# Recurrent attention and squared-ReLU FFN: stated issue order, two first solves stated side by side, inverses stored from GpSimd's queue

## The chip, the cores and the metric

The kernel runs on one core of a Trainium2 chip. The metric is the device time of one execution in microseconds (us), as a median of several runs. Every run has a state, fast or slow; verdicts here use fast runs alone. Each chip job ran the kernel before on the same chip beside the kernels under test, and its median lay between 1529.9 and 1535.5 us in all of them, so times of different jobs can be set side by side to about 0.3%.

## The reference

Attention of 4 sequences, 8 heads, 768 steps and head size 40, with a state that decays and is corrected at every step, and then an FFN over all 3072 tokens:

```python
# r, k, v, w, a, b: (4, 8, 768, 40) float32
for t in range(S):
    y[:, :, t] = einsum('bhd,bhde->bhe', rt, state)
    Sa = einsum('bhde,bhe->bhd', state, at)
    state = state * wt[:, :, None, :] - einsum('bhd,bhe->bhde', Sa, bt)
    state = state + einsum('bhd,bhe->bhde', vt, kt)
# tokens x: (3072, 320); moe_w_in: (320, 2048), moe_w_out: (2048, 320), float64
h = np.maximum(x @ w_in, 0.0)
return h * h @ w_out
```

The kernel cuts time into 6 rounds of 128 steps; a round has 4 chunks, one per sequence, 24 in all. A chunk has an early part (decays, and the matrix N of how steps correct each other), a remaining part (the products that don't need the state), and a chain (the state's part, which needs an inverse T built from N). The inverses of a round are found together in one "solve", a loop of 63 steps on 128 lanes. The FFN is woven into the chunks. The weights come as float64 and are unpacked to float32 on VectorE in 24 pieces of w_in and 16 of w_out.

## The kernel before

The solve takes an engine as argument: round 0's runs on VectorE, all others on GpSimd. Its loads and the store of the inverse are issued from SyncE, like nearly all transfers; the raw weights are fetched from ScalarE's queue.

```python
def solve(c, eng):
    ns = new("half_n", [128, HC, HC], 1)            # one buffer
    ts = new("half_t", [128, HC // 2, HC], 1)
    # ... clear ts, set its diagonal
    for par in range(2):
        for bb in range(B):
            for half in range(2):                    # 16 loads
                nc.sync.dma_start(out=ns[at:at + H], in_=kept_n[c * B + bb][rows, :, rows]...)
    yield
    for s in range(HC - 1):                          # 63 steps, two operations each
        eng.tensor_tensor(p_, ns[:, s, s + 1:]..., ts[:, :n, s:s + 1]..., Alu.mult)
        eng.tensor_tensor(ts[:, :n, s + 1:], ts[:, :n, s + 1:], p_, Alu.subtract)
        yield
    for par in range(2):
        nc.sync.dma_start(out=dst, in_=ts[par * 64:(par + 1) * 64])   # kept_t[c]
    yield
```

```python
# chain(i, g), first lines, when there is a state already
nc.vector.tensor_tensor(f_[:, :, 0], ended[bb], g["ends"][:, 0], Alu.mult)
nc.vector.tensor_copy(f_[:, :, 1], f_[:, :, 0])
nc.vector.tensor_tensor(f_, f_, same, Alu.mult)
nc.vector.tensor_tensor(st[:, :, :, :D], st[:, :, :, :D], f_..., Alu.mult)   # scale the state
for q in range(NP):
    nc.tensor.transpose(p_[...], st[:, q]..., ident)
```

```python
# the main loop
for i in range(len(order)):
    parts = [(chain(i, ready.pop(i)), 10)]
    # ... load(i + 1), rest(i + 1), the early part of chunk i + 8, weights, FFN steps
    weave(*parts)
    if bb == B - 1 and c + 2 < NCH:
        run(solve(c + 2, nc.gpsimd))
```

The order in which this is written isn't the order of issue: a scheduler moves instructions on each engine. So the weights, stated in the loop, are unpacked from 21 us on, before chunk 0.

## Time and profile before

| | before |
|---|---|
| median of 3 runs | 1534.52 us (1530.77 to 1537.87) |
| profiled span, granted clock | 1532.3 us, 0.786 |
| TensorE (PE) busy | 1062.4 us, 69% |
| VectorE (DVE) busy | 598.7 us, 39% |
| GpSimd (POOL) busy | 566.7 us, 37% |
| share of the chain that ended last | GpSimd 36%, TensorE 32% |

No engine is full. A busy share is a mean over stages with different limits.

### The profile page before, as it was taken

To read this page: it belongs to the slowest core of one execution; us is meant where nothing else is said; L and a number is where in the kernel's file an instruction comes from. 1 tells how busy PE (TensorE), PEld (TensorE's weight loads), DVE (VectorE), ACT (ScalarE), POOL (GpSimd) and SP (SyncE) were. 2 spreads that over 40 slices of the span, in tenths; PEclk is the share of its full clock that TensorE was granted. 3 is DMA by queue.
4 is the path that set the end of the run, shared out by engine and by line. 5 is a ranking of instruction groups with operands and counts; after the bars stand their busy time and mean duration, and the time that the engine had idled before them with its cause. 6 is when DMAs were issued, how large, how long until landed. Compare 5 with 4: busy or idle time off the path is not lost.

```text
span 1532.3 us, 18790 instructions
## 1 busy us (share of the span) xinstructions
PE 1062.4 (69%) x7248; PEld 884.2 (58%) x7248; DVE 598.7 (39%) x1330; ACT 202.1 (13%) x453; POOL 566.7 (37%) x702
## 2 busy tenths in 40 slices
PE   3300025009975989649989769899399994499999
PEld 2200014008854878537878658788278784388877
DVE  5887699604623243212135321346031342022311
ACT  0000001001210211101202101112012111021211
POOL 2110000009990079920199700499500899100000
PEclk9555555556897996859967878959799887699999
DMA  9634694374606677063846185654447640422100
GB/s 172 153 69 88 100 163 89 62 58 88 111 1 125 64 133 130 0 114 64 90 85 116 25 135 61 79 112 77 84 81 61 102 77 2 79 63 50 29 11 9
DMA packets 389881, 123.01 MB, mean 80 GB/s; under 512 B 318752, under 2 KB 372896, under 8 KB 389792
## 3 DMA queue, kind: packets, MB, share of 16 engines
q1 hardware_dynamic: 384000, 111.32, 45.6%
q10 hardware_dynamic: 5792, 10.49, 3.1%
q8 instruction: 57, 0.93, 0.3%
q14 instruction: 32, 0.26, 0.1%
HBM read 79.00 MB, written 41.78 MB: 79 GB/s over the span
## 4 chain that ended last, share of the span: by engine, by line
POOL 36%; PE 32%; DMA 11%; DVE 10%; SPq 7%; issue 4%; ACTq 0%; ACT 0%; DVEq 0%; POOLq 0%
PE ps_f L77 19%; POOL half_t L270 19%; POOL half_p L268 17%; PE ps_c L77 8%; PE ps_w L77 2%; DMA raw<-in_moe_w_in_dram 2%; SPq L262 2%; DMA in_k<-in_k_dram 2%; DMA raw<-in_moe_w_out_dram 2%; DVE half_t L270 2%; DVE half_p L268 2%; PE ps_w L202 2%; SPq L274 1%; SPq L398 1%; DMA kept_down<-down 1%
## 5 line engine op out<-in xcount | busy, mean ns | idle before, releaser
L268 POOL TENSOR_TENSOR half_p<-half_n,half_t 128x462 f32<-128x462 f32 (+46 forms) x315 | 255.6, 811 | 397.3 <-DMA in_k<-in_k_dram 176.1
L270 POOL TENSOR_TENSOR half_t<-half_t,half_p 128x462 f32<-128x462 f32 (+46 forms) x315 | 281.7, 894 | 24.7
L77 PE MATMUL ps_f<-tokens,w_in 128*128 128x256 f32 x1152 | 288.3, 399 | 0.5 <-DVE hid L416 0.5
L77 PEld LDWEIGHTS ps_f<-tokens,w_in 128*128 128x128 f32 x1152 | 217.7, 197 | 34.0 <-issue 1.5
L77 PE MATMUL ps_f<-w_out,hid 128*128 128x320 f32 x768 | 220.7, 441 | 0.0
L416 DVE TENSOR_TENSOR hid<-ps_f,hid 128x256 f32<-128x256 f32 x192 | 81.2, 423 | 319.2 <-ACT hid L415 319.0
L77 PEld LDWEIGHTS ps_f<-w_out,hid 128*128 128x128 f32 x768 | 144.4, 192 | 57.4 <-issue 3.0
L202 PE MATMUL ps_w<-ident,in_k 128*128 128x128 f32 x96 | 20.1, 342 | 151.0 <-DMA in_k<-in_k_dram 150.9
L77 PE MATMUL ps_c<-xr,T 64*64 64x40 f32 x768 | 65.8, 249 | 81.4 <-DMA T<-kept_t 74.5
L415 ACT ACTIVATE hid<-ps_f 128x256 f32<-128x256 f32 x192 | 73.6, 383 | 346.5 <-PE ps_f L77 346.5
L77 PEld LDWEIGHTS ps_c<-xr,T 64*64 64x64 f32 x768 | 59.1, 159 | 96.4 <-DMA T<-kept_t 75.0
L202 PEld LDWEIGHTS ps_w<-ident,in_k 128*128 128x128 f32 x96 | 14.2, 178 | 155.0 <-DMA in_k<-in_k_dram 117.7
L202 PE MATMUL ps_w<-ident,in_w 128*128 128x128 f32 x96 | 22.2, 376 | 113.9 <-DMA in_w<-in_w_dram 109.6
L77 PE MATMUL ps_w<-aT,bT 40*128 40x128 f32 x384 | 41.1, 352 | 76.3 <-DVE aT L239 76.3
L229 DVE TENSOR_TENSOR_SCAN up<-ps_w,ones 128x64 f32<-128x64 f32 x96 | 26.2, 273 | 170.9 <-PE ps_w L202 169.3
L253 POOL MEMSET half_t<- 128x2048 f32 x5 | 9.0, 1809 | 217.2 <-DMA kept_t<-half_t 217.2
L77 PEld LDWEIGHTS ps_w<-aT,bT 40*128 40x128 f32 x384 | 33.7, 244 | 86.0 <-issue 75.8
L202 PEld LDWEIGHTS ps_w<-ident,in_w 128*128 128x128 f32 x96 | 16.4, 199 | 115.5 <-issue 111.2
L244 ACT COPY N<-ps_w 128x512 f32<-128x512 f32 x48 | 25.8, 589 | 351.0 <-PE ps_w L77 284.0
L376 DVE TENSOR_TENSOR state<-ps_c,state 128x320 f32<-128x320 f32 x20 | 9.8, 491 | 126.2 <-PE ps_c L77 126.2
L218 DVE TENSOR_TENSOR RV<-ps_w,upper 128x512 f32<-128x512 f32 x48 | 30.9, 683 | 64.1 <-PE ps_w L77 64.1
L77 PEld LDWEIGHTS ps_c<-in_v,A 128*128 128x128 f32 x384 | 52.6, 215 | 2.4 <-ACT kvT L297 1.0
(182 smaller groups left out, 1475.2 us busy)
## 6 DMA issues: line engine op xcount, KB each, us to landing
kept_n<-N SPq DMA_DIRECT2D x48, 256.0 KB
half_n<-kept_n SPq DMA_DIRECT2D x96, 128.0 KB
kept_down<-down SPq DMA_DIRECT2D x24, 258.0 KB
kept_up<-up SPq DMA_DIRECT2D x24, 258.0 KB
kept_a<-aT SPq DMA_DIRECT2D x24, 256.0 KB
down<-kept_down SPq DMA_DIRECT2D x24, 256.0 KB
up<-kept_up SPq DMA_DIRECT2D x24, 256.0 KB
kept_t<-half_t SPq DMA_DIRECT2D x12, 512.0 KB
```

What stands on the lines that cost most here:

```text
L77: nc.tensor.matmul(o, l_, r_, start=start, stop=True, skip_group_check=True)
L202: nc.tensor.transpose(p_[:, q * 128:(q + 1) * 128], pair(x_, q), ident)
L218: nc.vector.tensor_tensor(t_, p_, over4(upper), Alu.mult)
L229: nc.vector.tensor_tensor_scan(up[:, q, MID + 1:C + 1], wT[:, q, MID:], ones, 1.0, Alu.mult, Alu.mult)
L244: nc.scalar.copy(t_, p_)
L262: nc.sync.dma_start(out=ns[at:at + H], in_=kept_n[c * B + bb][rows, :, rows].rearrange("s h t -> h s t"))
L268: eng.tensor_tensor(p_, ns[:, s, s + 1:].unsqueeze(1).to_broadcast([128, n, m_]), ts[:, :n, s:s + 1].to_broadcast([128, n, m_]), Alu.mult)
L270: eng.tensor_tensor(ts[:, :n, s + 1:], ts[:, :n, s + 1:], p_, Alu.subtract)
L274: nc.sync.dma_start(out=dst, in_=ts[par * 64:(par + 1) * 64])
L398: nc.sync.dma_start(out=t_[row:row + m_, j], in_=t_[at:at + m_, NT])
L415: nc.scalar.activation(h_, p_, Act.Relu)
L416: nc.vector.tensor_tensor(h_, p_, h_, Alu.mult)
```

## The change

The intent: every engine issues in the order in which the program states it, so that the author and not the scheduler decides what comes ahead of what; solves 0 and 1 are stated side by side (VectorE and GpSimd); the weights move from before chunk 0 into chunks 0 to 2; and the inverse is stored from GpSimd's own queue, so that SyncE doesn't wait for GpSimd. The core of the diff:

```diff
+    ctx.enter_context(tc.manual_schedule())
...
+    raws = [single(f"raw{i}", [128, WP, 2]) for i in range(2)]
+    def fetch_weights():
+        dst, srcs, cleared = pieces.pop(0)
+        raw = raws[len(pieces) % 2].bitcast(I32)[:, :dst.shape[-1]]
+        if cleared:
+            nc.gpsimd.memset(raws[len(pieces) % 2], 0.0)
         for row, m_, src in srcs:
             nc.scalar.dma_start(out=raw[row:row + m_]..., in_=src.bitcast(I32))
+        fetched.append((dst, raw))
...
-        ns = new("half_n", [128, HC, HC], 1)
+            ns = [new("half_n0", [128, Q, HC], 1), new("half_n1", [128, Q, Q], 1)]   # 32 loads, not 16
...
-        for par in range(2):
-            nc.sync.dma_start(out=dst, in_=ts[par * 64:(par + 1) * 64])
+        nc.gpsimd.dma_start(out=kept_t[c].rearrange(...), in_=flat)
...
-    weave((solve(0, nc.vector), HC + 1), (several(range(B, LEAD), prepare), 4 * B))
-    run(solve(1, nc.gpsimd))
-    run(rest(0, ready[0]))
+    # ... the 8 early parts, each a step ahead of the next
+    load(0)
+    fetch_weights()
+    first = rest(0, ready[0])
+    solving = [solve(0, nc.vector), solve(1, nc.gpsimd)]
+    for s_ in solving:
+        next(s_)                      # the loads of both
+    for _ in range(6):
+        next(first)
+    for s_ in solving:
+        run(s_)
+    run(first)
```

Smaller parts: decays are kept and loaded with their ends, T is loaded in 4 pieces, and a raw buffer is cleared only the first times a piece doesn't fill it (`cleared`).

More of the change, by code (lines that the diff above doesn't have):

```diff
@@ L137, with rounded @@
         nc.gpsimd.memset(same[e * DP:(e + 1) * DP, :, e:e + 1], 1.0)
-    middle = lambda t_: t_[:, :, MID:MID + 1]
-    ups = Ring("up", 1, [128, NP, C + 2], 1.0, middle)
-    downs = Ring("down", 1, [128, NP, C + 2], 1.0, middle)
+    whole = lambda t_: t_
+    ups = Ring("up", 2, [128, NP, C + 2], 1.0, whole)
+    downs = Ring("down", 2, [128, NP, C + 2], 1.0, whole)
     minus_x = Ring("minus_x", 2, [128, H, DP], 0.0, pads)
-    states = Ring("state", B, [128, NP, 2, DP], 0.0, lambda t_: t_)
+    states = Ring("state", B, [128, NP, 2, DP], 0.0, whole)
     w_in = single("w_in", [128, NT, DFF])
     w_out = single("w_out", [128, NF, DM])
-    def rounded(dst, srcs):
-        raw = work.tile([128, WP, 2], I32, tag="raw", name="raw")[:, :dst.shape[-1]]
-        n = 128
-        if sum(m_ for _, m_, _ in srcs) < n:
-            nc.gpsimd.memset(raw, 0)
+    WP = 320
+    WI = 256
+    raws = [single(f"raw{i}", [128, WP, 2]) for i in range(2)]
+    fetched = []
+    def fetch_weights():
+        if not pieces:
+            return
+        dst, srcs, cleared = pieces.pop(0)
+        raw = raws[len(pieces) % 2].bitcast(I32)[:, :dst.shape[-1]]
+        if cleared:
+            nc.gpsimd.memset(raws[len(pieces) % 2], 0.0)
         for row, m_, src in srcs:
             nc.scalar.dma_start(out=raw[row:row + m_].rearrange("p f e -> p (f e)"), in_=src.bitcast(I32))
+        fetched.append((dst, raw))
+    def rounded(dst, raw):
+        n = 128
         lo, hi = raw[:, :, 0].bitcast(U32), raw[:, :, 1]
@@ L172, in rounded, with weights @@
         nc.vector.tensor_tensor(dst, dst, rest, Alu.add)
-    WP = 320
-    WI = 256
-    pieces = [(w_in[:, j, f:f + WI], [(row, n, moe_w_in[o:o + n, f:f + WI]) for j_, row, o, n in places if j_ == j])
-              for f in range(0, DFF, WI) for j in range(NT)]
-    pieces += [(w_out[:, f, :], [(0, 128, moe_w_out[f * 128:(f + 1) * 128, :])]) for f in range(NF)]
-    def load_weights(n):
-        for _ in range(min(n, len(pieces))):
-            dst, srcs = pieces.pop(0)
-            if moe_w_in.dtype != FP32:
-                rounded(dst, srcs)
-                continue
-            if sum(m_ for _, m_, _ in srcs) < 128:
-                nc.gpsimd.memset(dst, 0.0)
-            for row, m_, src in srcs:
-                nc.scalar.dma_start(out=dst[row:row + m_], in_=src)
+    pieces = []
+    for j in range(NT):
+        for f in range(0, DFF, WI):
+            srcs = [(row, n, moe_w_in[o:o + n, f:f + WI]) for j_, row, o, n in places if j_ == j]
+            pieces.append((w_in[:, j, f:f + WI], srcs, f < 2 * WI and sum(n for _, n, _ in srcs) < 128))
+    pieces += [(w_out[:, f, :], [(0, 128, moe_w_out[f * 128:(f + 1) * 128, :])], False) for f in range(NF)]
+    def weights(n):
+        for _ in range(n):
+            if moe_w_in.dtype == FP32:
+                if pieces:
+                    dst, srcs, _ = pieces.pop(0)
+                    if sum(m_ for _, m_, _ in srcs) < 128:
+                        nc.gpsimd.memset(dst, 0.0)
+                    for row, m_, src in srcs:
+                        nc.scalar.dma_start(out=dst[row:row + m_], in_=src)
+            else:
+                fetch_weights()
+                if fetched:
+                    rounded(*fetched.pop(0))
+            yield
     kept_n = [dram.tile([C, H, C], FP32, tag=f"n{i}", name=f"kept_n{i}") for i in range(len(order))]
@@ L196 @@
     kept_down = [dram.tile([128, NP, C + 2], FP32, tag=f"dn{i}", name=f"kept_down{i}") for i in range(len(order))]
-    kept_t = [dram.tile([B, 2, H, HC, HC], FP32, tag=f"t{c}", name=f"kept_t{c}") for c in range(NCH)]
+    kept_t = [dram.tile([2, B, 2, H, HC // 2, HC], FP32, tag=f"t{c}", name=f"kept_t{c}") for c in range(NCH)]
     def turn(x_):
@@ L227, in early @@
         wT = turn(x_["w"])
+        yield
         for q in range(NP):
@@ L231, in early @@
         yield
+        bT_, aT_ = turn(x_["b"]), turn(x_["a"])
         nc.vector.reciprocal(down[:, :, MID + 1:C + 1], up[:, :, MID + 1:C + 1])
         nc.vector.reciprocal(up[:, :, :MID], down[:, :, :MID])
-        nc.sync.dma_start(out=kept_up[i][:, :, :C + 1], in_=up[:, :, :C + 1])
-        nc.sync.dma_start(out=kept_down[i][:, :, :C + 1], in_=down[:, :, :C + 1])
+        nc.sync.dma_start(out=kept_up[i], in_=up)
+        nc.sync.dma_start(out=kept_down[i], in_=down)
         yield
         bT, aT = turned("bT", 1), turned("aT", 1)
-        nc.vector.tensor_tensor(bT, turn(x_["b"]), down[:, :, 1:C + 1], Alu.mult)
-        nc.vector.tensor_tensor(aT, turn(x_["a"]), up[:, :, :C], Alu.mult)
+        nc.vector.tensor_tensor(bT, bT_, down[:, :, 1:C + 1], Alu.mult)
+        nc.vector.tensor_tensor(aT, aT_, up[:, :, :C], Alu.mult)
         nc.sync.dma_start(out=kept_a[i], in_=aT)
@@ L250, in solve @@
     def solve(c, eng):
-        ns = new("half_n", [128, HC, HC], 1)
-        ts = new("half_t", [128, HC // 2, HC], 1)
+        Q = HC // 2
+        if c > 0:
+            ns = [new("half_n0", [128, Q, HC], 1), new("half_n1", [128, Q, Q], 1)]
+            ts, prod = new("half_t", [128, Q, HC], 1), new("half_p", [128, 528], 1)
+        else:
+            room = w_out.rearrange("p f c -> p (f c)")
+            ns = [room[:, :Q * HC].rearrange("p (s t) -> p s t", s=Q),
+                  room[:, Q * HC:Q * HC + Q * Q].rearrange("p (s t) -> p s t", s=Q)]
+            ts = room[:, Q * HC + Q * Q:2 * Q * HC + Q * Q].rearrange("p (j t) -> p j t", j=Q)
+            prod = w_in[:, NT - 1, :528]
         eng.memset(ts, 0.0)
@@ L260, in solve @@
                 for half in range(2):
-                    rows = slice(half * HC, (half + 1) * HC)
-                    nc.sync.dma_start(out=ns[at:at + H], in_=kept_n[c * B + bb][rows, :, rows].rearrange("s h t -> h s t"))
+                    for n_, part in enumerate(ns):
+                        rows = slice(half * HC + n_ * Q, half * HC + (n_ + 1) * Q)
+                        cols = slice(rows.start, (half + 1) * HC)
+                        nc.sync.dma_start(out=part[at:at + H], in_=kept_n[c * B + bb][rows, :, cols].rearrange("s h t -> h s t"))
                     at += H
@@ L266, in solve @@
             n, m_ = s // 2 + 1, HC - 1 - s
-            p_ = new("half_p", [128, 528], 1)[:, :n * m_].rearrange("p (j t) -> p j t", j=n)
-            eng.tensor_tensor(p_, ns[:, s, s + 1:].unsqueeze(1).to_broadcast([128, n, m_]),
+            p_ = prod[:, :n * m_].rearrange("p (j t) -> p j t", j=n)
+            eng.tensor_tensor(p_, ns[s // Q][:, s % Q, s % Q + 1:].unsqueeze(1).to_broadcast([128, n, m_]),
                               ts[:, :n, s:s + 1].to_broadcast([128, n, m_]), Alu.mult)
@@ L271, in solve @@
             yield
-        for par in range(2):
-            dst = kept_t[c].rearrange("b f h (j two) t -> (b f h) two j t", two=2)[:, par]
-            nc.sync.dma_start(out=dst, in_=ts[par * 64:(par + 1) * 64])
+        nc.gpsimd.dma_start(out=kept_t[c].rearrange("two b f h j t -> (two b f h) (j t)"), in_=flat)
         yield
@@ L280, in rest @@
         x_ = loaded.pop(i)
-        up, down, aT = turned("up", 2), turned("down", 1), turned("aT_", 2)
-        ends = g["ends"] = new("ends", [128, 2, NP], 2)
-        nc.sync.dma_start(out=down, in_=kept_down[i][:, :, 1:C + 1])
+        up, down = new("up", [128, NP, C + 2], 2), new("down", [128, NP, C + 2], 1)
+        aT = turned("aT_", 2)
+        nc.sync.dma_start(out=down, in_=kept_down[i])
         nc.sync.dma_start(out=aT, in_=kept_a[i])
-        nc.sync.dma_start(out=up, in_=kept_up[i][:, :, :C])
-        with nc.allow_non_contiguous_dma(reason="two decays a head and channel"):
-            nc.sync.dma_start(out=ends[:, 0], in_=kept_down[i][:, :, 0])
-            nc.sync.dma_start(out=ends[:, 1], in_=kept_up[i][:, :, C])
+        nc.sync.dma_start(out=up, in_=kept_up[i])
+        ends = g["ends"] = new("ends", [128, NP], 3)
         g["up"], g["aT"] = up, aT
+        yield
         kT, rT = turned("kvT", 1), turned("rT", 2)
-        nc.vector.tensor_tensor(kT, turn(x_["k"]), down, Alu.mult)
+        nc.vector.tensor_tensor(kT, turn(x_["k"]), down[:, :, 1:C + 1], Alu.mult)
+        nc.vector.tensor_copy(ends, down[:, :, 0])
         yield
@@ L303, in rest @@
         for q in range(NP):
-            nc.tensor.transpose(p_[:, q * 128:(q + 1) * 128], down[:, q], ident)
+            nc.tensor.transpose(p_[:, q * 128:(q + 1) * 128], down[:, q, 1:C + 1], ident)
         inv = p_.rearrange("t (h d) -> t h d", h=H)[:, :, :D]
@@ L312, in rest @@
         g["T"], g["N"] = new("T", [128, H, HC], 2), new("N21", [HC, H, HC], 2)
+        nc.sync.dma_start(out=g["N"], in_=kept_n[i][:HC, :, HC:])
         for half in range(2):
-            nc.sync.dma_start(out=g["T"][half * HC:(half + 1) * HC], in_=kept_t[c][bb, half].rearrange("h j t -> j h t"))
-        nc.sync.dma_start(out=g["N"], in_=kept_n[i][:HC, :, HC:])
+            for par in range(2):
+                nc.sync.dma_start(out=g["T"][half * HC + par:(half + 1) * HC:2],
+                                  in_=kept_t[c][par, bb, half].rearrange("h j t -> j h t"))
         yield
@@ L328, in chain @@
             f_ = new("f", [128, NP, 2], 2)
-            nc.vector.tensor_tensor(f_[:, :, 0], ended[bb], g["ends"][:, 0], Alu.mult)
+            nc.vector.tensor_tensor(f_[:, :, 0], ended[bb], g["ends"], Alu.mult)
             nc.vector.tensor_copy(f_[:, :, 1], f_[:, :, 0])
@@ L377, in chain @@
             ended[bb] = new(f"end{bb}", [128, NP], 2)
-            nc.vector.tensor_copy(ended[bb], g["ends"][:, 1])
+            nc.vector.tensor_copy(ended[bb], g["up"][:, :, C])
             yield
@@ L394, in chain @@
         t_ = tokens[i // GB][:, :, n * C:(n + 1) * C]
-        nc.vector.tensor_tensor(t_, y_, g["up"], Alu.mult)
+        nc.vector.tensor_tensor(t_, y_, g["up"][:, :, :C], Alu.mult)
         for j, row, h, d, m_ in gaps:
@@ L405, in ffn @@
         for gi in range(len(order) // GB):
-            while gi not in gathered:
+            while gi not in gathered or len(pieces) + len(fetched) > NF:
                 yield False
@@ L418, in ffn @@
                 yield True
+            while pieces or fetched:
+                yield False
             for n in range(GB):
@@ L435 @@
     gathered = set()
-    PER_CHUNK = -(-(NF + 4 * GB) // GB)
+    STEPS = NF + 4 * GB
     def run(gen):
@@ L450, in weave @@
             run(gen)
-    def several(n, f):
-        for i in n:
-            if i < len(order):
-                yield from f(i)
     def prepare(i):
@@ L460, in prepare, with filler @@
         yield from early(i)
-    def weights(n):
-        while n:
-            load_weights(1)
-            n -= 1
+    def filler(n):
+        for _ in range(n):
+            next(second, None)
             yield
-    def filler(n):
-        while n and next(second):
-            n -= 1
-            yield
+    firsts = [prepare(i) for i in range(LEAD)]
+    for i in range(LEAD + 1):
+        if i == 0:
+            next(firsts[0]), next(firsts[0])
+            continue
+        now, then = firsts[i - 1], firsts[i] if i < LEAD else iter(())
+        next(now)
+        next(then, None)
+        next(now)
+        next(then, None)
+        run(now)
     ready = {0: {}}
-    run(several(range(B), prepare))
     load(0)
-    weave((solve(0, nc.vector), HC + 1), (several(range(B, LEAD), prepare), 4 * B))
-    run(solve(1, nc.gpsimd))
-    run(rest(0, ready[0]))
+    fetch_weights()
+    first = rest(0, ready[0])
[7 more added lines that the diff above has]
+    run(first)
     for i in range(len(order)):
@@ L484 @@
             ready[i + 1] = {}
-            parts.append((rest(i + 1, ready[i + 1]), 6))
+            parts.append((rest(i + 1, ready[i + 1]), 7))
         if i + LEAD < len(order):
-            parts.append((prepare(i + LEAD), 4))
-        if pieces:
-            parts.append((weights(20), 20))
-        parts.append((filler(PER_CHUNK), PER_CHUNK))
+            parts.append((prepare(i + LEAD), 5))
+        if pieces or fetched:
+            n = len(pieces) + len(fetched) - NF if i < GB else NF
+            n = -(-n // (GB - i)) if i < GB else n
+            parts.append((weights(n), n))
+        parts.append((filler(STEPS // GB + 1), STEPS // GB + 1))
         weave(*parts)
```

## The prediction

> **What bounds the kernel now.** I read the page first, then the chain that ended last, then tables by stretch, then the timelines of SyncE's queue, VectorE and TensorE. From the page, the chain's shares by engine:
>
> ```profile
> POOL 36%; PE 32%; DMA 11%; DVE 10%; SPq 7%; issue 4%; ACTq 0%; ACT 0%; DVEq 0%; POOLq 0%
> ```
>
> GpSimd, busy for 37% of the span, carries as much of the chain as TensorE, busy for 69%. So no engine is full: the two take turns. The table by stretch shows where (span, busy us of PE, PEld, DVE, ACT, POOL, granted clock, DMA share, GB/s):
>
> ```profile
> 76.00:197.50 121.50, 5.15 (x28) 3.96 (x28) 94.44 (x283) 1.07 (x2) 6.62 (x13) 0.50 0.49 91
> 197.50:293.50 96.00, 28.99 (x168) 25.19 (x168) 90.28 (x196) 5.98 (x11) 0.00 (x0) 0.53 0.52 99
> 293.50:344.00 50.50, 0.00 (x0) 0.00 (x0) 0.00 (x0) 0.00 (x0) 2.11 (x3) 0.50 0.76 71
> 552.00:638.00 86.00, 81.00 (x634) 69.16 (x634) 41.49 (x79) 16.64 (x37) 79.96 (x78) 0.84 0.51 97
> 638.00:672.00 34.00, 0.04 (x1) 0.00 (x0) 0.42 (x1) 0.61 (x2) 20.38 (x34) 0.54 0.28 51
> 1318.00:1484.00 166.00, 161.72 (x1204) 132.16 (x1204) 39.97 (x76) 31.44 (x72) 0.00 (x0) 0.96 0.22 46
> ```
>
> Until 294 us VectorE is the bound (early parts, weights, solve of round 0). Then all wait 50 us for the store of the inverse, the loads for the next solve, and T. From 344 us the rounds repeat (GpSimd's solves end at 461, 659, 874, 1092, 1310): period about 217 us, in which TensorE runs well, then dry. SyncE's queue says why (start, us, what):
>
> ```profile
> 603.42 0.65 SPq L314 DMA_DIRECT2D T<-kept_t  x1
> 658.65 2.71 SPq L274 DMA_DIRECT2D kept_t<-half_t  x2
> ```
>
> For 55 us the queue stands on the inverse's store, which waits for GpSimd; every later load is behind it. The loads of a solve hold the queue too, 31.22 / 14 = 2.23 us each (2.41 in the quiet stretch at 298 us):
>
> ```profile
> 500.30 31.22 SPq L262 DMA_DIRECT2D half_n<-kept_n  x14
> ```
>
> In the tail, without solves, TensorE is full at clock 1.00, and a chunk takes 35.5 us from one decay transpose to the next:
>
> ```profile
> 1383.21 0.66 PE L304 MATMUL ps_w<-ident,down 128*128 128x128 f32 x4
> 1418.66 0.65 PE L304 MATMUL ps_w<-ident,down 128*128 128x128 f32 x4
> ```
>
> **What the Trainium skill says.** SBUF — State Buffer, "Who interferes with whom": a VectorE instruction with two SBUF inputs contends with a GpSimd instruction that reads SBUF, and the loser waits the whole instruction out. The trace agrees: the same two-input operation on 8 elements, without and with a solve on GpSimd:
>
> ```profile
> 247.94 0.15 DVE L331 TENSOR_TENSOR f<-f,same 128x8 f32<-128x8 f32 x1
> 358.33 0.69 DVE L331 TENSOR_TENSOR f<-f,same 128x8 f32<-128x8 f32 x1
> ```
>
> Around 358 us such operations lose 0.41 to 0.54 us each, at 417 up to 0.85; I take 0.56. DMA: Bandwidth & Descriptors, "Why a DMA increments its semaphore by 16 and not by 1": the outermost dimension sets how many of the 16 DMA engines serve a transfer; these loads have 8 (heads). The DMA share of 0.52 to 0.8 beside them fits. The same page, "Anatomy of one DMA — SWDGE (gpsimd) path": about 2.0 us + bytes / 436e3 from GpSimd's queue; for the 1 MB inverse an estimate of 4.4 us. The trace of before has no large transfer from there. TensorE: Matmul & The Clock Gate, "What's actually happening": idle halves the clock until some microseconds of work; agrees (0.54 in the dry stretch, 1.00 in the tail).
>
> **The change part by part**, from the instruction streams of the changed kernel, built but not run.
>
> *Early parts, 8 chunks.* VectorE per chunk: 8 scans 1.5 us, 2 reciprocals 3.3, 2 products 1.3 = 6.1 (5.4 to 11.4 us of before). A chunk moves about 1.8 MB; at the 162 to 212 GB/s that before shows when its DMA is full, 8.5 to 11 us; its packets are longer now (2 KB rows for decays), so I take 8.4, DMA-bound: 8 x 8.4 + 8 = 76 us.
>
> *Loads of both solves.* Each 64x64 load is split in two, to skip a quarter of it: 64 loads, of as many rows as the 32 before. Estimate from 2.23 to 2.41 us per pair, a little off for shorter rows: 2.1 x 32 = 68 us. In SyncE's order they all stand before the first decay load of chunk 0's remaining part, and in VectorE's order that part's six products stand before the solve. So the solve can't start before 76 + 3 + 68 = 148 us plus that part's chain (5 matrix steps at the cold clock, copies, masks), 14 us: 162 us.
>
> *Solves.* On VectorE: busy 64.93 us in 126 operations, and 0.035 between two: 69 us, to 231. The "side by side" does not come about: in GpSimd's order the store of round 0's inverse, which waits for VectorE, stands before the first operation of round 1's solve. So GpSimd starts at 231, not beside it. Store (4.4 + its issue) and T loads: 9 us; chunk 0 begins at 240 us, against 344.
>
> *Weights.* They now lie in chunks 0 to 2, on VectorE, beside GpSimd's solve. A w_in piece takes 2.8 us (20.76 to 23.57), of which four operations have two SBUF inputs: 2.8 + 4 x 0.56 = 5.0. Twelve a chunk and about 13 us of VectorE's other work. Two pieces precede chunk 0's wait: to 249 us; then 10 x 5.0 + 13 = 63, to 312; chunk 1: 12 x 5.0 + 14 = 74, less 7 since the solve (117 us + about 15 for the contention) ends at 366: 379. Chunk 2: 16 w_out pieces at 3.3 = 53, + 13, + 16 x 0.42 of the FFN, + 4 for late fetches: 77, to 456. Chunk 3 is TensorE's, 38: 494. Before had ended chunk 3 near 455, so here the change is behind by some 40 us.
>
> *Rounds 1 to 5.* A chunk on TensorE: 35.5 (tail) + 2.3 for an early part (12 transposes, 16 small products) = 38 us where there is one, 35.5 where not. The store no longer holds SyncE. But in stated order the 32 loads of solve c+2 stand at each round's start, after T and before the next chunk's k: 34 us + 1 + 5 (k and decays landing), in which TensorE has some 6 us of chain and FFN work. 34 + 6 - 6 + 1 for re-warming = 35 us dry, at four starts (after chunks 3, 7, 11, 15). A round: 4 x 38 + 35 = 187 us against 217. GpSimd's loop: loads 37, solve 117 + 5, store 6, T 4 = 169 < 187: not the bound.
>
> *Sum.* 494 + 12 x 38 + 8 x 35.5 + 4 x 35 = 1374. Tail: the last two chunks' FFN, 38.4 us at full clock (96 x 0.217 + 64 x 0.274, tail of before), and 6 for latency and the output: 1418, say **1420 us**.
>
> **The rivals.** (1) *TensorE isn't dry at the round starts*, if SyncE gets ahead of it: 4 x 35 away, 1280. For it: before ran on for 40 us beyond such loads. Against: there the scheduler put FFN work in between; the stated order has matrix work of the next chunk's k first. (2) *The weights cost more*: if every two-input operation waits out a full GpSimd operation (1.1 us at mid-solve) and fetches come late behind ACT's copies, chunks 0 to 2 take 60 us more: 1480. For it: waits of 0.85 us at mid-solve. Against: the mean of all is lower. (3) *Strict order costs TensorE a wait at many steps*, which halves the clock too: 42 instead of 38 us a chunk, 1500, as good as the same. For it: the clock fell to 0.66 in parts of 570 to 600 us. Against: the tail ran a like order full. (4) *GpSimd's loop becomes the bound*, if split loads cost per load: 64 x 2.23 at start (+75), and 71 a round: period 206: together +150, slower than before. Against: a load of half the rows has half the descriptors per DMA engine.
>
> **Range and chances.** The terms that may err: weights +-35, the dry starts -60/+40, chunk length 20 x -1/+3, start +-20. They are partly independent: 1345 to 1500. Faster by over 2% means below 1504: 0.86. Within 2%: 0.10. Slower: 0.04.
>
> **What would show each step.** T of chunk 0 landing near 240 us; GpSimd's first solve operation after the store, not near 150; VectorE's two-input weight operations at about 1 us while GpSimd solves, 0.42 after; VectorE nearly full in chunks 0 to 2, TensorE not, to about 456; SyncE's queue in 32 loads of about 1.06 us at four round starts, with TensorE dry for about 35 us; rounds of 187 us; no stretch in which SyncE stands on the store. It is wrong if the rounds take 210 us or more, if TensorE's clock stays under 0.8 in them, or if the weights run past 500 us.

## The result, and the profile after

| | before | after |
|---|---|---|
| median | 1532.64 us (4 runs, 1528.92 to 1537.87) | 1606.67 us (4 runs, 1602.88 to 1609.7) |
| ratio | | 1.0479, 95% interval 1.0438 to 1.052 |
| profiled span, clock | 1532.3 us, 0.786 | 1608.0 us, 0.787 |

The kernel became slower by nearly 5%. A ratio is the mean time of one kernel's fast runs over that of the other's fast runs of the same rounds, so it isn't quite the ratio of the medians.

On the page, the chain that ended last has changed hands (shares of the span by engine):

```profile
PE 52%; issue 15%; DVE 10%; SPq 9%; POOL 8%; DMA 5%; ACT 0%; ACTq 0%; DVEq 0%; POOLq 0%
```

(SPq and ACTq are the queues from which SyncE and ScalarE issue transfers.) GpSimd fell from 36% to 8%: it no longer sets the rounds. The time was lost in other places, and three of them can be read off the trace.

**The start.** In the table by stretch (span, then busy us of PE, PEld, DVE, ACT, POOL, granted clock, DMA share, GB/s) there is a stretch in which GpSimd alone works:

```profile
240.00:312.00 72.00, 0.00 (x0) 0.00 (x0) 0.00 (x0) 0.00 (x0) 67.06 (x64) 0.50 0.00 0
```

The prediction had VectorE full of weights there and chunk 0 ending at 312 us. T had come early, and solve 1 had begun right behind the store (timelines of GpSimd and of TensorE: start, us, engine, line, operation; `w_out` here is round 0's inverse, as its solve works in the room of weights that aren't unpacked yet):

```profile
216.59 0.68 POOL L305 DMA_DIRECT2D kept_t<-w_out  x1 [204.66 <-DVE power L176]
217.35 0.29 POOL L301 TENSOR_TENSOR half_p<-half_n,half_t 128x63 f32<-128x63 f32 x1
...
224.26 1.90 PE L78 MATMUL ps_c<-xr,T 64*64 64x40 f32 x16 [76.58 <-DMA T<-kept_t]
```

The timeline of all engines at the end of that solve shows what the others were waiting for:

```profile
334.22 0.60 POOL L305 DMA_DIRECT2D kept_t<-half_t  x1 [0.31 <-POOL half_t L303]
334.81 0.65 POOL L165 MEMSET raw<- 128x640 f32 x1
335.50 2.81 ACTq L167 DMA_DIRECT2D raw<-in_moe_w_in_dram  x4
338.35 0.42 ACT L387 COPY minus_x<-ps_c 64x320 f32<-64x320 f32 x1 [190.22 <-DMA raw<-in_moe_w_in_dram]
338.82 1.92 PE L78 MATMUL ps_c<-minus_x,N 64*64 64x40 f32 x16 [111.63 <-ACT minus_x L387]
```

Read it from below. TensorE stood 112 us for a copy of ScalarE. ScalarE stood because the fetch of a weight piece is ahead of that copy in its order. The fetch stood because the second raw buffer had to be cleared first. The clearing takes 0.65 us, on GpSimd, and is stated behind the whole of solve 1; VectorE waits for the piece. The Trainium skill says of the queues in PSUM — Partial Sum Buffer, "Engine vs sequencer instructions": "ScalarE/VectorE/GpSimdE queues are strict FIFO." The trace agrees: 0.65 us of work came 117 us late, and three engines stood for it.

**The round starts.** SyncE's queue at the start of a round, and TensorE in the same stretch:

```profile
562.63 2.59 SPq L347 DMA_DIRECT2D T<-kept_t  x4
...
566.47 28.87 SPq L295 DMA_DIRECT2D half_n<-kept_n  x32
595.45 0.88 SPq L114 DMA_DIRECT2D in_k<-in_k_dram  x1
```

```profile
PE ps_w L221 <- DMA in_k<-in_k_dram: 121.3, 6, 29.4
```

The second fence is from the list of waits (us in total, times, longest). TensorE waits up to 29.4 us for the next chunk's k, because 32 loads of a later solve are ahead of it. This is as predicted.

**Every chunk's start.** TensorE's timeline at the start of a chunk inside a round, and the waits on the line that scales the state:

```profile
900.76 0.67 PE L78 MATMUL ps_f<-tokens,w_in 128*128 128x256 f32 x2 [1.87 <-DMA tokens<-tokens]
...
906.63 0.95 PE L369 MATMUL ps_c<-ident,state 128*128 128x128 f32 x4 [3.44 <-DVE state L365]
```

```profile
  PE ps_c L369: 49.7, 20
```

In stated order the scaling stands on VectorE behind products of the FFN (`hid`), which wait for TensorE, which waits for a gather of tokens. So VectorE reaches the scaling late, and TensorE stands for it once a chunk: 49.7 us in 20 times, and the granted clock falls after such a stand (here to 0.50 from 908 to 910 us, and back to 1.00 from 912).

| end of chunk (its product with the decays, us) | predicted | after |
|---|---|---|
| 0, 1, 2, 3 | 312, 379, 456, 494 | 376, 433, 505, 557 |
| length of chunks 4, 5, 6, 7 | 73, 38, 38, 38 | 71, 49, 43, 51 |
| 23, and the end | 1374, 1418 | 1562, 1608 |

A round takes 214 us (chunks 4 to 7), and the last weight piece is unpacked from 518 us on: two of the prediction's three signs of being wrong, "210 us or more" and "past 500 us".

### The profile page after: what moved, and what is told of

Same layout as the page of the kernel before. It is cut to its first block, busy times and chain, and to the rows that moved or that the text cites. A ratio compares the mean times of both kernels' runs of the same rounds, so it can differ in the third digit from the quotient of the medians.

```text
span 1608.0 us, 18792 instructions
## 1 busy us (share of the span) xinstructions
PE 1052.2 (65%) x7248; PEld 866.0 (54%) x7248; DVE 601.0 (37%) x1354; ACT 201.0 (13%) x453; POOL 562.9 (35%) x692
## 4 chain that ended last, share of the span: by engine, by line
PE 52%; issue 15%; DVE 10%; SPq 9%; POOL 8%; DMA 5%; ACT 0%; ACTq 0%; DVEq 0%; POOLq 0%
PE ps_f L78 29%; PE ps_c L78 13%; SPq L295 7%; PE ps_w L78 5%; POOL half_t L303 4%; POOL half_p L301 3%; PE ps_w L221 3%; DMA in_k<-in_k_dram 2%; SPq L431 1%; DMA raw<-in_moe_w_in_dram 1%; DMA tokens<-tokens 1%; DVE signed L180 1%; PE ps_c L369 1%; DVE power L184 1%; DMA raw<-in_moe_w_out_dram 1%
## 5 line engine op out<-in xcount | busy, mean ns | idle before, releaser
L78 PE MATMUL ps_f<-tokens,w_in 128*128 128x256 f32 x1152 | 326.1, 431 | 46.0 <-DMA tokens<-tokens 25.6
L78 PEld LDWEIGHTS ps_f<-tokens,w_in 128*128 128x128 f32 x1152 | 234.4, 215 | 90.9 <-DVE hid L449 22.1
L78 PE MATMUL ps_c<-minus_x,N 64*64 64x40 f32 x384 | 29.3, 237 | 111.7 <-ACT minus_x L387 111.6
L321 DVE TENSOR_TENSOR kvT<-ps_w,down 128x512 f32<-128x512 f32 x24 | 16.6, 691 | 221.0 <-DMA down<-kept_down 142.6
L78 PEld LDWEIGHTS ps_c<-minus_x,N 64*64 64x64 f32 x384 | 26.4, 145 | 121.5 <-ACT minus_x L387 112.5
L176 DVE TENSOR_SCALAR power<-raw 128x256 int32<-128x256 int32 (+1 forms) x40 | 11.8, 296 | 130.1 <-DMA raw<-in_moe_w_in_dram 127.1
L78 PE MATMUL ps_c<-in_v,A 128*128 128x40 f32 x384 | 59.0, 324 | 0.0
L237 DVE TENSOR_TENSOR A<-ps_w,upper 128x512 f32<-128x512 f32 x48 | 30.9, 685 | 72.2 <-PE ps_w L78 72.2
L78 PE MATMUL ps_w<-rT,kvT 40*128 40x128 f32 x384 | 33.5, 310 | 32.4 <-DVE RX L237 31.6
L369 PE MATMUL ps_c<-ident,state 128*128 128x128 f32 x80 | 17.9, 364 | 49.7 <-DVE state L365 49.7
```

The lines of the kernel that those rows point to most:

```text
L78: nc.tensor.matmul(o, l_, r_, start=start, stop=True, skip_group_check=True)
L237: nc.vector.tensor_tensor(t_, p_, over4(upper), Alu.mult)
L321: nc.vector.tensor_tensor(kT, turn(x_["k"]), down[:, :, 1:C + 1], Alu.mult)
L369: nc.tensor.transpose(p_[:, q * 128:(q + 1) * 128], st[:, q].rearrange("p e d -> p (e d)"), ident)
```

## The experiments

Twelve kernels ran; all gave correct results. "After" is the changed kernel, 1606.67 us.

| kernel | median us | ratio to before | 95% interval |
|---|---|---|---|
| e1_clear | 1552.77 | 1.0093 | 1.0022 to 1.0165 |
| e2_state | 1545.79 | 1.0078 | 1.0038 to 1.0118 |
| e3_late | 1497.48 | 0.9768 | 0.9734 to 0.9803 |
| e4_sched | 1370.5 | 0.8936 | 0.8891 to 0.898 |
| e5_three | 1383.03 | 0.9016 | 0.8968 to 0.9063 |
| e6_sched_sync | 1504.71 | 0.9804 | 0.9763 to 0.9845 |
| e7_before_pool | 1470.7 | 0.9577 | 0.9538 to 0.9615 |
| e8_clear_side | 1556.16 | 1.0135 | 1.007 to 1.02 |
| e9_all | 1386.09 | 0.9025 | 0.8993 to 0.9057 |
| e10_store_sync | 2027.77 | 1.3202 | 1.3153 to 1.3251 |
| e11_all_before | 1363.74 | 0.8901 | 0.8862 to 0.8939 |
| e12_half_after | 1337.34 | 0.871 | 0.8673 to 0.8746 |

The medians are of all runs. One run of e1 and one of e12 was slow; their fast runs have medians of 1548.23 and 1334.27 us.

### e1_clear: the clearing alone

```diff
+    for t_ in raws:
+        nc.gpsimd.memset(t_, 0.0)     # once, at the start
     fetched = []
...
-        if cleared:
-            nc.gpsimd.memset(raws[len(pieces) % 2], 0.0)
```

> Both raw buffers are cleared at setup; nothing else changes. Theory A (the second clearing stands behind round 1's solve in GpSimd's order and holds ScalarE, and with it all, from 226 to 338 us): chunk 0 goes on at about 227 us, 112 us earlier; the weights then run beside the solve, each w_in piece at about 5.0 us in place of 2.8 to 3.5, which gives back 35 to 50 us: 1530 to 1545 us. Rival B (VectorE's weights bound the start anyway and the gap only moves): less than 20 us gained, above 1585. Rival C (the shared port costs nothing): the whole 112 us, 1495.

1552.77 us, 54 us less than after; the fast runs alone, 1536.15 to 1557.31, have a median of 1548.23, 58 less. That is 3 us above the range that the first theory gave, and far from the rival's 1585. The profiled run is the fastest. The chunks show the effect undiluted: chunk 0 now ends at 305 us in place of 376 and chunk 3 at 495 in place of 557. The stretch that was empty is full:

```profile
240.00:312.00 72.00, 22.02 (x130) 19.28 (x129) 69.07 (x80) 1.66 (x3) 67.30 (x61) 0.52 0.11 35
```

The same run measures what a weight piece costs beside a solve. VectorE's timeline, first at mid-solve, then after the solve's end:

```profile
259.40 1.12 DVE L177 TENSOR_SCALAR power<-power 128x256 int32<-128x256 int32 x1
...
261.70 0.28 DVE L179 TENSOR_SCALAR signed<-raw 128x256 int32<-128x256 int32 x1
262.01 1.16 DVE L180 TENSOR_TENSOR signed<-signed,power 128x256 int32<-128x256 int32 x1
...
351.63 0.29 DVE L177 TENSOR_SCALAR power<-power 128x256 int32<-128x256 int32 x1
...
352.49 0.43 DVE L180 TENSOR_TENSOR signed<-signed,power 128x256 int32<-128x256 int32 x1
```

Not only the operations with two inputs wait for GpSimd, as I had counted, but most of those with one as well: eight of a piece's nine last 1.1 to 1.4 us. From the start of one piece (258.25) to that of the state's product after it (268.19) it is 9.9 us, where the prediction had 5.0.

### e2_state: the scaling of the state alone

```diff
     # rest(i): the remaining part, a chunk ahead
         nc.vector.tensor_copy(ends, down[:, :, 0])
+        if c > 0:
+            # the four operations that scale the state, moved here from chain(i)
```

> The state of a chunk is scaled a chunk ahead, beside its decays, so that VectorE no longer does it behind the first FFN product of the chunk. Theory (in stated order this is a wait at every chunk's start, 3.4 us for TensorE, and the half clock after it): 20 x 3.4 us, plus some 2 us each for the clock, gone: 1500 to 1540 us, chunks inside a round 43 us in the mean, not 47.5. Rival (the gather of the tokens holds TensorE at the same place): less than 25 us gained, above 1580.

1545.79 us: 61 us less than after, 6 us above the range. Chunks 5 to 7 take 44, 42 and 46 us in place of 49, 43 and 51, chunks 9 to 11 take 44, 40 and 47 in place of 53, 42 and 47. TensorE has no wait left for the scaling in the stretch from 671 to 962 us; its transposes of the state start without one (timeline of TensorE):

```profile
837.49 0.60 PE L371 MATMUL ps_c<-ident,state 128*128 128x128 f32 x4
```

The waits were 50 us; the other 11 fit the clock, which these stands held down, but no run separates that.

### e3_late: the loads of the next solve later

```diff
-        if bb == B - 1 and c + 2 < NCH:
-            run(solve(c + 2, nc.gpsimd))
...
+        # in the next round's first chunk, as one more woven part
+        if bb == 0 and 0 < c and c + 1 < NCH:
+            parts.append((late(c + 1), STEPS // GB + 1))   # 5 empty steps, then the solve
```

> The solve of round c+2 and its 32 loads are stated five steps into the next chunk, behind that chunk's own loads, not in front of them. Theory (TensorE is dry for 29 us at four round starts because k and the decays queue behind 32 loads): about 4 x 29 = 115 us gone, rounds of 185 us: 1490 to 1510 us. Rival (GpSimd's loop of loads, solve, store and T, then about 180 us, becomes the bound, or the loads hold up the queue as much in their new place): 40 us or less gained, above 1565.

1497.48 us, 109 us less than after, within the range, and 2.3% less than before (unclear by the 2% rule). The round from chunk 4 to 7, first of after, then of this kernel (table by stretch):

```profile
557.00:771.00 214.00, 172.16 (x1242) 142.07 (x1240) 71.84 (x150) 34.05 (x77) 110.39 (x130) 0.86 0.47 87
```

```profile
563.00:753.00 190.00, 174.16 (x1266) 144.18 (x1262) 73.99 (x153) 35.07 (x79) 110.10 (x130) 0.93 0.52 99
```

The same work on TensorE in 24 us less, at clock 0.93 in place of 0.86. So it was the order in SyncE's queue that dried TensorE, not the time that the loads take.

### e4_sched: the scheduler's order, all else as changed

```diff
-    ctx.enter_context(tc.manual_schedule())
```

> The stated order is taken off and the scheduler orders the engines as in the kernel before; the rest of the change stays. Theory (the strict order costs: clearing behind the solve, loads in front, waits at chunk starts; the store from GpSimd's queue is the good part, as SyncE no longer stands on it for 55 us a round): faster than the changed kernel and than before, 1400 to 1500 us. Rival (the scheduler puts T's loads or the store in front of others and the queue stands again): 1530 or more.

1370.5 us, 30 us below the theory's range: the stated order as it was written costs 236 us, and the rest of the change is worth 162 us against before.

### e5_three: the edits of e1, e2 and e3 together, in stated order

> The three single edits (both raw buffers cleared at the start; the state scaled in the remaining part; the next solve's loads later) together, in stated order. Alone they took 54, 61 and 109 us off the changed kernel's 1607. Theory (they act on different stretches, so they add): 1607 - 54 - 61 - 109 = 1383, between 1360 and 1410, rounds of about 170 us. Rival (GpSimd's loop becomes the bound: solve 117, store 5, then the loads only some 15 us into the next chunk and 30 us long): rounds of 180 us or more and 1420 to 1450 us, TensorE waiting for T at each round's start.

1383.03 us, as the sum has it: the three edits give back 224 us. That this is near the 236 us of e4 doesn't show that these places are what stated order costs, since the two kernels gain in different stretches. Chunk 3 ends at 427 us in e4 and at 503 in e5 (557 in after), and the 20 chunks behind it take 898 and 833 us (1005). In e4 the scheduler has 17 weight pieces unpacked before 132 us, ahead of the solves, which no edit of e5 does. In its rounds SyncE's queue still stands on the inverse, now with the loads of T, which wait for the store (list of waits of e4):

```profile
SPq L346 <- DMA kept_t<-half_t: 119.0, 5, 43.6
```

In e5, from 640 to 1200 us, TensorE is nearly full:

```profile
640.00:1200.00 560.00, 518.52 (x3884) 429.22 (x3883) 210.55 (x428) 103.04 (x234) 354.63 (x428) 0.95 0.50 94
```

TensorE waited for T 13 us in all in the rounds, so GpSimd's loop isn't the bound, though there is little room left.

### e6_sched_sync and e7_before_pool: what the queue of the store is worth

```diff
 # e6_sched_sync: on top of e4_sched
-        nc.gpsimd.dma_start(out=kept_t[c]..., in_=flat)
+        nc.sync.dma_start(out=kept_t[c]..., in_=flat)
 # e7_before_pool: in the kernel before
-            nc.sync.dma_start(out=dst, in_=ts[par * 64:(par + 1) * 64])
+            nc.gpsimd.dma_start(out=dst, in_=ts[par * 64:(par + 1) * 64])
```

> The scheduler's order (1370 us) with the inverses stored from SyncE's queue again. Theory (the store's queue is what made the rest of the change worth 162 us): SyncE stands on the store beside each solve as before, every later load behind it, TensorE dry for some 30 us in each of 4 rounds: 1480 to 1530. Rival (the scheduler puts the store late enough, and the gain came from the start and the weights): under 1400.

> The kernel before with only its inverses stored from GpSimd's queue. Theory: SyncE's 55 us of standing and TensorE's dry stretch of 34 us (638 to 672 us) go in each of 4 to 5 rounds: 1370 to 1430. Rival (GpSimd's loop of loads, solve, store and T sets the round, so the dry stretch only moves to a wait for T): 1490 to 1535.

e6 gave 1504.71 us, as the theory has it: under the scheduler the store's queue is worth 134 of the 162 us. SyncE's queue stands on the store in all five of GpSimd's solves (list of waits of e6, 280 to 1300 us):

```profile
SPq L304 <- POOL half_t L302: 212.4, 5, 47.3
```

e7 gave 1470.7 us, in the gap between both: the store alone brings the kernel before 4.2%, 62 us and so about half of what the theory expected; neither range holds it. The list of waits of e7, over the same stretch, names what took the place of the store:

```profile
SPq L262 <- POOL half_p L268: 104.3, 3, 54.0
SPq L314 <- DMA kept_t<-half_t: 65.5, 2, 41.7
```

L262 is the load of the next solve's N. Before has one buffer for it, so the load waits until GpSimd's running solve has read the last row, and everything behind it in SyncE's queue waits too; before has this wait once, for 50.7 us, beside the store's. L314 is a load of T, which waits for the store, as in e4. The changed kernel has two smaller buffers for N; in e4 the wait for them isn't among the seven longest of SyncE's queue. That the buffers and nothing else remove it is argued, not shown: no run changed them alone.

### e8_clear_side: the solves truly side by side

```diff
 # on top of e1_clear
-        nc.gpsimd.dma_start(out=kept_t[c]..., in_=flat)
+        (nc.gpsimd if c else nc.scalar).dma_start(out=kept_t[c]..., in_=flat)
```

> The edit of e1_clear (1553 us) and round 0's inverse stored from ScalarE's queue, so that GpSimd's solve no longer stands behind VectorE's: the two solves truly side by side. Theory (the two engines hold each other up where both read two operands from SBUF): VectorE's solve takes 110 to 140 us in place of 69, chunk 0 starts some 50 us later than the 216 us of e1, and what the weights win by an idle GpSimd (24 pieces by about 2 us) gives that back: 1540 to 1570. Rival (little holding up): VectorE's solve 75 us or less, 1490 to 1510.

1556.16 us, as the theory has it, and no better than e1. The two engines hold each other up (timeline of both; VectorE's operations are the ones on `w_in` and `w_out`):

```profile
189.62 1.47 POOL L303 TENSOR_TENSOR half_t<-half_t,half_p 128x504 f32<-128x504 f32 x1
190.02 1.56 DVE L301 TENSOR_TENSOR w_in<-w_out 128x450 f32<-128x450 f32 x1
191.17 1.35 POOL L301 TENSOR_TENSOR half_p<-half_n,half_t 128x525 f32<-128x525 f32 x1
191.61 1.39 DVE L303 TENSOR_TENSOR w_out<-w_out,w_in 128x450 f32<-128x450 f32 x1
```

Each record starts about 0.4 us after the other engine's and ends about 0.4 us after it; VectorE's operation on 450 elements takes 1.4 to 1.6 us, and 0.63 in after, where GpSimd stands. VectorE's solve ran from 149 to 284 us, 135 us in place of 71, and GpSimd's from 138 to 277, 139 in place of 117. The prediction had the loser wait the whole instruction out. That isn't what this shows: both solves were done in 146 us, and one after the other they take 71 + 117 = 188, so the operations overlap in part. Side by side, both solves were done at 284 us; in e1, one after the other, at 334, but the first at 212 already, and chunk 0 needs only the first. So it cost nothing that the change did not bring the two side by side, which the prediction had seen.

### e10_store_sync: stated order with the store from SyncE

```diff
 # in the changed kernel
-        nc.gpsimd.dma_start(out=kept_t[c]..., in_=flat)
+        nc.sync.dma_start(out=kept_t[c]..., in_=flat)
```

> The changed kernel with the inverses stored from SyncE's queue again, in stated order. Theory (stated order makes the queue of the store decisive): in each of the four rounds in which a solve stands, SyncE stands on the store for the whole solve, 117 us, with every load of the next chunk behind it; the start loses nothing, as GpSimd may then solve beside VectorE: 1607 + 4 x 117 = 2075, less some 50 at the start: 2000 to 2080. Rival (a chunk's loads were ahead already): under 1800.

2027.77 us (2 runs), in the range. SyncE's queue:

```profile
526.38 29.33 SPq L295 DMA_DIRECT2D half_n<-kept_n  x32
676.93 0.34 SPq L305 DMA_DIRECT2D kept_t<-half_t  x1
677.37 0.40 SPq L114 DMA_DIRECT2D in_k<-in_k_dram  x1
```

From 556 to 677 us nothing is issued: the next chunk's k is behind the store, and the store is behind the solve. A scheduler had blunted this to 55 us in before by putting other work ahead; stated order needs the other queue.

### e9_all, e11_all_before, e12_half_after: a better start

```diff
 # on top of e5_three
     solving = [solve(0, nc.vector), solve(1, nc.gpsimd)]
-    for s_ in solving:
-        next(s_)
+    next(solving[0])                      # e12 (e9 and e11: as before)
+    run(weights(2 * DFF // WI))           # e11 and e12: 16 pieces
     for _ in range(6):
         next(first)
+    run(weights(2 * DFF // WI))           # e9 only: here in place of above
+    next(solving[1])                      # e12
     for s_ in solving:
         run(s_)
```

> The kernel of e5_three (1383 us) with 16 of the 24 pieces of w_in unpacked on VectorE before the solves, where it waited 69 us for the solves' loads. Theory (in e5 a piece beside GpSimd's solve takes some 10 us, so the weights hold chunks 0 to 2): the 16 pieces take 16 x 3.4 = 54 us of the idle 69, chunks 0 and 1 take some 53 us each and chunk 3 ends near 453 in place of 503: 1383 - 50 = 1333, between 1320 and 1350. Rival (GpSimd's loop takes over, so rounds of over 180 us give it back, or the fetches slow the solves' loads): 1365 or more.

e9 gave 1386.09 us, no gain, and not for the rival's main reason. The pieces ran at 147 to 197 us, since VectorE stood at the first product of chunk 0's remaining part (timeline of VectorE):

```profile
137.25 0.69 DVE L321 TENSOR_TENSOR kvT<-ps_w,down 128x512 f32<-128x512 f32 x1 [75.28 <-DMA down<-kept_down]
```

Its decays are behind all 64 loads in SyncE's queue. I had made the mistake of the change itself: put work behind a wait that it doesn't need.

> The kernel of e9_all with the 16 pieces moved up one place, ahead of the six steps of the first remaining part. In e9 they stood behind that part's first product, which waits for a load queued behind all 64 loads of the solves, so they ran at 147 to 197 us and not in the idle stretch. Theory: now they run at about 66 to 125 us, VectorE's solve starts at 147 as in e5 (1383 us), and chunk 3 ends 48 us earlier than in e9 (495): 1386 - 48 = 1338, between 1322 and 1352. Rival (the start isn't what limits it, GpSimd's solves are): 1370 or more.

e11 gave 1363.74 us: 22 us less than e9, not 48, and outside both ranges. The pieces now ended at 122 us, but the first solve's loads, 30 us long in after, took 67 us beside the fetches (SyncE's queue, and its waits):

```profile
67.32 66.80 SPq L295 DMA_DIRECT2D w_out<-kept_n  x32
134.16 32.43 SPq L295 DMA_DIRECT2D half_n<-kept_n  x32
...
SPq L295 <- DMA raw<-in_moe_w_in_dram: 32.5, 10, 7.5
```

The skill says in DMA: Bandwidth & Descriptors, "Issuing engines are not separate DMA queues", that transfers started by different engines run on the same 16 DMA engines and interleave. That fits, but from 67 to 134 us 84 GB/s were moved, at a DMA share of 0.47, and 218 GB/s in the first 76 us of the same run. So the bandwidth alone hardly explains it, and what holds the loads stays open.

> The kernel of e11 (1364 us) with the 32 loads of GpSimd's first solve moved behind the first chunk's decays and the six steps of its remaining part, so that VectorE's solve waits for its own 32 loads alone. In e11 those 32 loads took 32 us of SyncE's queue ahead of the decays (134 to 167 us), and VectorE's solve began at 184. Theory (this step of the prediction, 68 us of loads ahead of solve 0, is half avoidable): the solve begins near 152, chunk 3 ends 32 us earlier than in e11 (484), and the time is 1364 - 32 = 1332, between 1320 and 1346. Rival (the moved loads delay GpSimd's solve 1 or the T loads and it is paid back in chunks 0 to 4): 1352 or more.

e12 gave 1337.34 us (fast runs 1334.27), within the range, though 26 (29) and not 32 below e11. The first solve's loads still took 68 us beside the fetches. The same product of the remaining part comes 33 us earlier than in e11 (141.57 in place of 174.77 us), and chunk 3 ends at 453 us in place of 484:

```profile
141.57 0.69 DVE L321 TENSOR_TENSOR kvT<-ps_w,down 128x512 f32<-128x512 f32 x1 [18.78 <-DMA down<-kept_down]
```

This is the fastest kernel, 12.9% below before; its interval doesn't touch that of e4.

## Why the prediction was wrong

It said 1420 us (1345 to 1500) and gave "slower" 0.04; 1606.67 came. The profile's 1608 us are 190 above 1418. Of these, 63 lie before the end of chunk 3 (557 for 494), 125 in the 20 chunks after it (1005 for 880), and 2 in the tail (46 for 44).

**The step that failed first: the weights in chunks 0 to 2, "beside GpSimd's solve".** The prediction placed each piece on VectorE and asked what an operation costs there, and never followed a piece's own inputs back through the other engines' orders. The clearing of the second raw buffer stands behind the solve on GpSimd, and the fetch behind it holds ScalarE. So no piece but the first could be unpacked until 338 us. e1_clear shows it by taking it away: chunk 3 then ends at 495, where the prediction has 494. That agreement is partly luck. Two terms of that step were wrong and cancel: a piece beside a solve takes 9.9 us at mid-solve and not 5.0 (rival (2) had named the two-input operations' part of that), and the solve ended at 334 and not at 366, since it began at 213 and not at 231 and took 121 us and not 132.

**The step that failed second: "a chunk on TensorE: 35.5 + 2.3".** Chunks within a round took 42 to 53 us. The 35.5 came from before's tail, where a scheduler had ordered the work. Rival (3) named the mechanism, a wait at many steps that halves the clock, and priced it at 42 us a chunk and 1500; I set it at too low a chance because "the tail ran a like order full". e2_state shows that one wait, of the state's scaling behind the FFN's products, was 57 of the 125 us (its 20 chunks took 948). Of the other 68, 50 lie in the 12 chunks with an early part, some 4 each. Part of that is work: in e5 the chunk from 808 to 852 us has TensorE busy for all of its 43.7 us at clock 1.00, and the one behind it for 35.9 us of 38.4 at 0.96, so a chunk with an early part holds some 40 us of work (an estimate from these two), not 38. The rest is waits and clock, which no run separates.

**Right:** the store stands in GpSimd's order before solve 1, which began at 217.35 behind it. VectorE's solve took 71 us (145 to 216) for 69, store and T 7.7 us for 9, and T reached TensorE at 224 for 240. The store from GpSimd's queue, put at 4.4 us, took 4.2 to 6.0 us from its issue to the clearing that waits for it (719.22 to 723.60 us in one of the three rounds that show it). The loads took 61 us for 68, and the early parts had issued their last store at 62 us, for 76. That a DMA share of 0.52 to 0.8 "fits" 8 of 16 engines was no test: the share can pass 1 (1.06 from 20 to 38 us of before), so it doesn't count engines, and no run here does. The dry starts were right in place, number and cause: 29 us of wait for 35, and 71 us for the first chunk of a round against 73; e3_late takes them away and gives 109 us back, of the 4 x 29 = 116 us. GpSimd's loop was not the bound: it waited 461 us for its loads. In the rounds SyncE no longer stands on the store, and e10_store_sync shows what it would have cost.

**Where the expected gain went.** It is there: with the scheduler's order the rest of the change gives 162 us (e4_sched), 134 of them by the queue of the store (e6_sched_sync). The stated order took 236 us away again. The three places above are worth 224 when mended in stated order (e5_three), but the scheduler gained its 236 partly elsewhere, with weights ahead of the solves, and lost some in the rounds. How the 236 divide is open, as is the part of the clock in e2's 61.

## What to carry to other kernels

When order is fixed by hand, follow every input of every piece of work back through each queue that it passes: a 0.65 us clearing stated behind a 117 us solve stopped three engines, and a load stated behind 32 others dried TensorE. State small things that others wait for (clearing, scaling, decays) ahead of the long things that nobody needs yet, and test it by moving them one at a time; here the gains simply added. And don't take a duration from a stretch that a scheduler ordered as the price of the same work in your own order.

## What the Trainium skill lacked or had wrong

- SBUF — State Buffer, "Who interferes with whom": it says that `tensor_scalar` can enter a two-port mode and then contends with GpSimd as well. That fits here, and the prediction, which counted only operations with two inputs, had missed it: four of a piece's five one-input operations took 1.1 to 1.3 us beside a solve and 0.29 after it (e1_clear). After it, a copy of 4 elements takes 0.16 us and a two-input operation on 256 takes 0.43, so the one-input ones pass about two elements in the time of one (an estimate from these three). What the section lacks is why the fifth was spared, at 0.28 us beside the solve.
- The same section has no price for two engines that both read two SBUF inputs for long, nor how far two such operations overlap: VectorE's solve went from 71 to 135 us, GpSimd's from 117 to 139, both together 146 (e8_clear_side).
- PSUM — Partial Sum Buffer, "Engine vs sequencer instructions": the queues are called strict FIFO, but that a transfer which waits to be issued holds the compute behind it in the same queue isn't said there. Here ScalarE had no operation for 190 us, and TensorE waited 112 of them for its copy.
- DMA: Bandwidth & Descriptors, "Issuing engines are not separate DMA queues": it lets transfers of several queues interleave, and has no figure there for what one queue's loads lose. Here 32 loads went from 30 to 67 us beside weight fetches, at a DMA share of 0.47 (e11_all_before).
